# Layer norms written as (x - mean) * rsqrt everywhere, with a new stored order

## The chip, the cores and the metric

The kernel runs on one core of one Trainium2 chip. Its time is device microseconds per execution, and lower is better. A core has five engines that run side by side: TensorE (PE, matmuls, with its weight loads shown as PEld), VectorE (DVE), ScalarE (ACT), GpSimd (POOL) and SyncE (SP, which here issues nearly all the DMAs). They wait for one another through semaphores alone. TensorE writes into eight PSUM banks, and all other tiles lie in SBUF, 128 partitions wide.

## The reference

A transformer block whose two norms are modulated by a condition vector `c`. With S = 2048 tokens and D = 448, it computes

```
sa, ca, ga, sb, cb, gb = split(silu(c) @ w_mod, 6)
h = layernorm(x) * (1 + ca) + sa
x = x + ga * attention(h)            # 16 heads of 28, causal, window of 256 keys
h = layernorm(x) * (1 + cb) + sb
z = gelu(h @ w_in)                   # 448 -> 1792
z1, z2 = z[:, :896], layernorm(z[:, 896:])
x = x + gb * ((z1 * (w_sp @ z2 + b_sp)) @ w_out)      # w_sp is 2048 x 2048
```

where `layernorm(v) = (v - mean) / sqrt(var + 1e-5)` along the last axis, with no gain or offset of its own. Inputs and output are bf16.

## The kernel before

The 2048 tokens are 16 tiles of 128 rows (`NT`). All stages run interleaved on all engines.

- First norm (`ln1`). The tiles are grouped in blocks of 1, 1, 2, 4, 4 and 4 (`BLOCKS`). For each tile VectorE computes statistics (`bn_stats`, named `l1_<t>st0`) and aggregates them to mean and variance (`l1_<t>ag`, into `mv_all`). For each block one operation adds epsilon (`l1_<t0>ve`, into `ve_all`, VectorE) and one raises to the power -0.5 (`l1_<t0>rs`, into `rs_all`, GpSimd). From the second block on a further operation makes -mean * rsqrt (`l1_<t0>nm`, into `nm_all`, VectorE). The norm of a tile (`xn<t>`, into `xn`) then runs on one of the engines that its list of options has: on VectorE as subtract and multiply, on GpSimd as multiply and add of `nm_all`, on ScalarE as an Identity activation with scale and bias.
- Transposing the normed tiles to hT: for the first three blocks by matmuls against an identity (`tr<b>_...`), evicted with the modulation (`hT<b>_<u>`); for the three blocks of four tiles by DMA transposes on SP's queue (`hx<t>`, line 717), followed by the modulation in place (`hm<b>_<c>`, line 707), four of them to a block, each on an engine of choice.
- Projections (`qk<b>_<g>`, `v<t>`), evicted by ScalarE or VectorE (`qke<b>_<g>`, `ve<t>`); scores (`S...`), exponentials on ScalarE (`E...`, line 887), masks on GpSimd (`M...`, line 890), the product with V (`PV...`), and per tile on VectorE or GpSimd a transpose, a reciprocal and a scaling (`oq<j>`, `rec<j>`, `nrm<j>`, `oT<j>`); then the output projection (`wo<j>`) and its addition to x (`x1_<j>`).
- Second norm (groups of 4, 4, 4, 2 and 2 tiles): the same statistics and the same helper `ln_rs`, with `l2_<j0>nm` always; the norm itself (`x2_<j>`) in the multiply-and-add form on all three engines; DMA transposes (`h2T<j>`), modulation (`h2q...`, `h2m...`).
- The gated MLP: `z2m`, `z1m` (matmuls), `z2g`, `z1g` (gelu on ScalarE), the third norm per tile (`l3_<t>...`, `z2n<t>`, already in the subtract-and-multiply form), then `G<tb>_<ft>_<qd>` (the product with w_sp, whose transposed blocks are loaded by `wsp<tb>_<p>`), and `out`, `fin`, `st`. Matmuls on 64 of 128 rows (names that end in `_r`) can run two at a time when the two use opposite halves and stand next to each other.

What sets the order. Every operation is declared with its dependencies and its options (engine, cost). Nothing is planned when the kernel is built: `ORDER` is a text that lists all operations by number in their order of issue, with the option taken after a dot (none is the first) and the buffers or banks taken after a slash. `Planner.schedule` reads it; each engine then runs its own operations in that order, each waiting for what it depends on. So an operation that waits holds back everything behind it on its engine, SP's DMAs too. TensorE's operations are of several shapes of its array (whole, 32 columns wide, 28 or 64 rows high), and neighbours in the order share a shape where they can.

Of the kernel before, what the change touches and what calls it, by code (L numbers as in the profile page):

```python
# [179 lines left out]
1 34 32 31 0 2 3 4 8 11 23 27 22 33 24 25 28 21 29 1693/0 1694 1695 1696 1697 1698 36 35 37/0 1699 1700 1701 15 67 38 1702 39 40/6 41 42 43 26 68 69  # L180
70 71/2 44 45 46 47 48 49 50 51 52 53 54 55 72/0 76/7 56 73 77.1 78/2 79.1 1703 74/4 1704 57.1 75 6 65.1 60.1 7 61.1 5 64.1 1705 1706 1707 1708 1709
12 18 10 9 62.2 125 126 127 63.2 58.2 180 182 128 129 181 95/7 96 85/0 90/1 91 80/2 105/3 81 86 115/6 106 97 98 82 87 88 92 93 99 83 89 94 116 107 117
118 119 108 109 130/2 133/4 134 131/7 183 66 184 1710 84.1 496/0,0 498/1 1711 1712 132.1 150/1 135/0 165/2 140/3 141 136 151 152 59.2 137 153 154 166
138 167 142 168 139 143 144 251 169 110/2 111 100/3 112 113 114 101 102 103 104 145/1 146 147 148 149 155/3 156 157 158 160/0 161 159 162 163 164
497/1,1 501/9 170/2 171 172 173 185 186 188.1/0 187.1/3 189/1 190 192/3 193 194 30.1 247 245 249 246 248 252 250 253 254 120/6 121 122 123 174.1
513/0,1 514/4 517/6 175/2 176 177 13 19 14 494/3 178 179 191.1 255 256/0 124.1 332 225/1 215/0 227 226 218 228 229 520/1,0 523/5 521/7 217 16 17 495
20 260 195/2 198 197 196 199.1 205/1 206 216 219.1 207 208 209.1 330 333 328 334 331 329 335 336 200/3 202 203 201 204 220/2 221 223 222 224 230/0 231
# [12 lines left out]
668 666 664 375.1 401/1 665 675/0 676 404 403 694/3 696/2,1 697 402 405.1 677/1 626/0 627 628 629 630 946 953.1/1 699 698 700 454/1 701/0,2 705/0 455  # L200
456 457 458.1 674/0 669 671 673 672 670 684/0 706/1 702/2 703/4 708/1,2 709/1 678/1 391/1 394 392 393 395.1 685 686/0 449/0 451 450 710/0 704 707
711/1,0 714 715 712 713 679/1 687/2 680 681 682 683 961 464/3 466 444/2 465 467.1 468.1 452.1 453 447.1 746/0,1 748/4 917 918 911 1428 1425 954 916
446 445 448.1 727/0 434/1 726 722 725 723 724 747/2 749/1,2 752 949/0 947/1 737/0 951/2 962 738 436 435 437 438.1 739.1/1 750 751 753 688/0 689 690
691 692 740/2 959 963 964 965 960 754/0,2 755/3 459/1 719/0 462.1 718 721 460 720 756/0 758/1 759/2 757 760 761/1,0 762/0 763/5 966 461 463.1 479/2
481 469/3 472 470 716 717 728/0 729 967 482 480 483 764/1,0 765 471 473.1 484/0 486 485 439/1 487 488.1 441 767 799/2,1 800/3 730.1/0 731/0 921 1426
919 920 910 950 952 948 1432 1431 909 1429 440 442 443.1 766 768 801/1 956.1 769/0 773 770 772 771 774 781/0 968 958 955 957 802/0,2 805 806 741/1 742
782 732/0 733 734 735 736 969 783/0 976.1/0 977 803 804 807/2,1 743 744 778/0 780 775 745 784/0 811/4 812/1 808/2 809/0 813 814/1,0 816/4 776 777 779
790/0 791 785/1 786 787 788 789 792/1 815/0 817/0,2 818 1433 1436 810 820 474/0 475 477 476 478.1 931/1 852/0,1 854/5 853/2 825/0 823 822 826 1035/2
1036 1037 793/1 935 794/3 795 934 819 824 821 827 834/0 796 797 798 835 932 933 1038 1043.1 970/0 971 974/2 972/1 973 855/0,1 858 856 1052/0 1053 1054
1069/3 1071 1039/2 1070 1040 1041 1072 1077.1 1042 1044 982 984 986 988 1055 1060.1 857 836.1/0 859 837/2 860/0,1 1090/3 1056/1 1091 1092 830/0 833  # L210
489/2 490 491 1057 1058 831 864/3 865/4 861/2 866 862/1 863 1093 1095.1 492.1 493.1 1059 1061.1 867/0,1 868/1 975 978.1 828 829 832 843/0 838/3 839
840 841 1086/1 1087 1088 842 987 985 989 983 990 991 869/3 1073/0 1074 1089 1076 1094.1 870/2,0 873 1430 1434 1438 871 1096/0 844 980 845/0 979 1075
846/2 1078 981.1 992 995/2 996 999.1/1 993.1/0 1000 994 1295/6 1305/7 1296 1307 1306 1300/3 1297 1301 1154/0 1150 1302 1330/1 1332 1333 1298 1303 1304
1153 1308 1309 1157 847/2 848 1005 1156 849 1155 850 851 1006 1007 1331 1151 1152 1103/1 1104 1158/2 872 874 879/0 1107/2 1340/7 876 880 875 878 877
1109 1097 1008 1009 887/0 1160 1335/4 1337 1110 1338 1343 1106 1334 1299 1079/1 997/2 888 1010 1011 1098 1080 1081 1159 998 1014/1 889.1/0 1015 1315/1
885/0 1105 1108 1112.1 1111.1 1336 1339 882 883 1317 1320/6 1012.2/0 1013 881 1316 1321 884 1310/0 1312 886 1453 1451 1441 1440 1445 1442 890/2 896/0
897 1082 1161 1162 898/0 1083 1120/0 1342 1124 1322 1325/3 1127 1318 1319 1313 1123 1323 1328 891/0 892 1341 893 894 895 1125 1290/1 1126 1326 1344
1324 1121 1122 1291 1311 1128/3 1002.2 1314 1004.1 1084 1163 1099 899/0 900/0 901 902 1292 1020 1001 903 904 1164 1085 1370/7 1180/0 1181 1327 1375/6
1371 1182 1003.2 1045/1 1329 1365/0 1376 1366 1184 1186 1185 1293 1294 1368 1373 1378 1187 1183 1188/2 1372 1367 1380/3 1350/1 1381 1369 1377 1374
1379 1382 1355/2 1199/0 1357 1195 1197 1285/0 1286 1356 1200 1165/1 1169 1172 1198 1383 1288 1353 1358 1202 1168 1170 1196 1201 1171 1021 1016 1022  # L220
1017.2 1100 1130 1023 1024 1129 1101 1025 1131 1026 1029.2/0 1384 1027.1/2 1102 1132 1133 1046 1047 1048 1049 1028 1134 1190 1189 1191 1359 1203/0
1167 1352 1287 1166 1345/3 1360/2 1214/0 1215 1210 1216 1212 1351 1173/3 1289 1354 1211 1361 1225/1 1229 1019.1 1050 1018.1 1348 1217 1363 1228 1051
1192 1205 1030 1455 1034.2 1213 1232 1218/1 1227 1362 1226 1032.1 1031.1 1385/0 1230 1347 1364 1033.1 1259/0 1193 1175 1204 1174 1219 1194 1176 1177
1220 1178 1179 1206 1221 1222 1207 1208 1223 1255 1346 1349 1231 1257 1260 1233/2 1386 1387 1395/2 1397 1390/3 1391 1135/1 1139 1062/3 1064 1235 1224
1209 1063 1065 1066 1388 1389 1142 1393 1138 1258 1262 1392 1394 1261 1256 1137 1405/1 1141 1410/0 1140 1136 1143/1 1412 1400/3 1401 1407 1396 1411
# [72 lines left out]
def bass_adaLN_cond__sliding_block__mixer_gmlp__prompt_kernel(  # L298
# [14 lines left out]
    FH = 896  # L313
# [300 lines left out]
    def ln_rs(name, prio, slot, t0, n, deps, nm):  # L614
# [4 lines left out]
        if not nm:  # L619
            return r  # L620
# [19 lines left out]
    def ln1(b, pr):  # L640
# [8 lines left out]
        for t in range(t0, t0 + n):  # L649
# [12 lines left out]
            if b:  # L662
                opts += [("pool", pool2_ns(512), f_p)] + ([("act", act_ns(512), f_a)])
# [640 lines left out]
```

## Time and profile before

| | us |
|---|---|
| median of three runs | 265.88 (265.82 to 266.1) |
| the profiled execution | 265.4 |
| its span, from the first instruction to the last | 263.7 |
| TensorE busy in it | 257.2 |
| VectorE busy | 164.3 |
| ScalarE busy | 128.8 |
| GpSimd busy | 95.2 |

The profile is one execution. A line of a group reads: source line, engine, operation, out<-in, shapes, count, then busy time and mean duration in ns, then idle time of the engine just before and what ended it. A line of a timeline reads: start, length (both us), engine, line, operation, count, and in brackets the idle time before it with the engine that ended it. Names are the program's tiles, so operations of different names can share a line (707 is a modulation, 630 a norm in the multiply-and-add form, 631 one in the subtract-and-multiply form, 616 the epsilon addition, 617 the power, 621 and 647 the l_nm operations). SPq is SP's queue of DMA issues.

### The profile page before, as it was taken

The numbers are of one execution on the slowest core, as the hardware profiler recorded it, in microseconds if no ns is written. First come the engines' busy times: TensorE is split into PE (matmuls) and PEld (weight loads), VectorE is DVE, ScalarE is ACT, GpSimd is POOL, SyncE is SP. The second block draws the span as 40 slices with busy tenths as digits, with TensorE's granted clock in tenths as the row PEclk, the third lists the DMA queues.
The fourth block names the chain that finished last, engine by engine and source line by source line (L and its number), as shares of the span: only waits on it lengthen the run. The fifth ranks groups of instructions, "written<-read, shape, count | busy, mean of one in ns | idle before, by whom it ended". The sixth has DMA issues, their size and how long they took to land.

```text
span 263.7 us, 7760 instructions
## 1 busy us (share of the span) xinstructions
PE 257.2 (98%) x3395; PEld 128.7 (49%) x3395; DVE 164.3 (62%) x387; ACT 128.8 (49%) x183; POOL 95.2 (36%) x148
## 2 busy tenths in 40 slices
PE   6999999999999999999999999999999999999996
PEld 2675455655455554543434444444444444444453
DVE  4798988788989997979587702352514213344453
ACT  4899999999999999778888000000000000000000
POOL 3594968878878776515331300000000000000000
DMA  6975560256994764768899400000000000000043
GB/s 225 357 193 120 145 163 5 62 125 145 227 114 118 118 87 101 85 130 154 144 199 222 92 2 0 0 0 2 0 0 0 2 0 0 0 2 17 0 142 119
DMA packets 61022, 23.86 MB, mean 91 GB/s; under 512 B 49854, under 2 KB 60861, under 8 KB 60989
## 3 DMA queue, kind: packets, MB, share of 16 engines
q1 hardware_dynamic: 60715, 22.92, 40.0%
q8 instruction: 26, 0.43, 0.6%
q10 hardware_dynamic: 274, 0.46, 0.5%
q14 instruction: 7, 0.06, 0.1%
HBM read 9.47 MB, written 1.84 MB: 43 GB/s over the span
## 4 chain that ended last, share of the span: by engine, by line
PE 91%; DVE 3%; POOL 2%; ACT 1%; DMA 1%; issue 1%; SPq 0%; DVEq 0%; POOLq 0%
PE ps L467 80%; PE ps L464 11%; DVE hT L707 1%; DMA hT<-xn 1%; ACT arena L887 1%; POOL xn L630 1%; POOL arena L890 0%; ACT WQK L734 0%; DVE x_sb L1077 0%; SPq L717 0%; DVE QKT L820 0%; ACT hT L693 0%; PE ps L779 0%; DVE xn L630 0%; DVE o_sb L1063 0%
## 5 line engine op out<-in xcount | busy, mean ns | idle before, releaser
L887 ACT ACTIVATE arena<-ps 128x1024 bf16<-128x1024 f32 x76 | 72.4, 1028 | 2.0 <-PE ps L467 1.4
L1212 DVE TENSOR_TENSOR tmpg<-ps,bsp_bc 128x512 bf16<-128x512 f32 x28 | 19.2, 689 | 60.2 <-PE ps L467 59.9
L467 PE MATMUL ps<-QKT,z 128*128 128x512 bf16 x224 | 52.1, 379 | 0.0
L890 POOL TENSOR_SCALAR_AFFINE_SELECT arena<-arena 128x512 f32<-128x512 f32 x60 | 39.1, 669 | 12.2 <-ACT arena L887 9.5
L467 PEld LDWEIGHTS ps<-QKT,z 128*128 128x128 bf16 x224 | 21.9, 98 | 26.4
L617 POOL TENSOR_TENSOR rs_all<-ve_all,neghalf 128x1 f32<-128x1 f32 (+2 forms) x27 | 18.9, 703 | 33.1 <-DVE ve_all L616 32.9
L467 PE MATMUL ps<-w_spD,z 128*128 128x512 bf16 x112 | 27.9, 379 | 0.0
L467 PE MATMUL ps<-w_spC,z 128*128 128x512 bf16 x112 | 27.8, 379 | 0.0
L467 PE MATMUL ps<-hT,w_in_sb 128*128 128x512 bf16 (+1 forms) x97 | 25.3, 380 | 0.0
L467 PE MATMUL ps<-w_in_sb,hT 128*128 128x448 bf16 (+1 forms) x102 | 24.6, 353 | 0.0
L467 PE MATMUL ps<-w_out_sb,z1T 128*128 128x448 bf16 (+2 forms) x119 | 22.0, 341 | 0.0
L609 DVE BATCH_NORM_STATS2 st_all<-z2raw 128x6 f32<-128x448 bf16 x32 | 18.7, 616 | 4.9 <-ACT z2raw L1135 3.9
L467 PE MATMUL ps<-hT,WQK 128*128 128x128 bf16 (+4 forms) x124 | 19.9, 291 | 0.1
L609 DVE BATCH_NORM_STATS2 st_all<-x_sb 128x6 f32<-128x448 bf16 x32 | 18.6, 608 | 0.0
L467 PE MATMUL ps<-QKT 28*64 28x64 bf16 (+3 forms) x944 | 17.7, 210 | 0.6 <-ACT arena L887 0.3
L1154 ACT ACTIVATE z1T<-ps 128x512 bf16<-128x512 f32 x28 | 15.9, 597 | 4.3 <-PE ps L467 4.2
L467 PE MATMUL ps<-arena,Vaug 128*32 128x128 bf16 x720 | 17.7, 221 | 0.0
L467 PEld LDWEIGHTS ps<-w_spC,z 128*128 128x128 bf16 x112 | 11.0, 98 | 13.2
L467 PEld LDWEIGHTS ps<-w_spD,z 128*128 128x128 bf16 x112 | 11.0, 98 | 13.0
L467 PEld LDWEIGHTS ps<-QKT 28*128 28x128 bf16 (+1 forms) x944 | 11.3, 97 | 11.7 <-ACT arena L887 5.9
L630 POOL TENSOR_SCALAR xn<-x_sb,rs_all,nm_all 128x512 bf16<-128x512 bf16 x20 | 15.4, 781 | 4.0 <-DVE nm_all L647 1.7
L467 PEld LDWEIGHTS ps<-w_out_sb,z1T 128*128 128x128 bf16 x119 | 11.6, 98 | 10.1
(93 smaller groups left out, 331.7 us busy)
## 6 DMA issues: line engine op xcount, KB each, us to landing
wmod_sb<-in_w_mod_dram SPq DMA_DIRECT2D x8, 224.0 KB, 3.8
w_in_sb<-in_B_w_in_dram SPq DMA_DIRECT2D x8, 224.0 KB, 4.0
out_dram<-fin SPq DMA_DIRECT2D x16, 112.0 KB, 1.7
x_sb<-in_A_x_dram SPq DMA_DIRECT2D x3, 448.0 KB, 8.1
bsp_bc<-in_B_b_sp_dram SPq DMA_DIRECT2D x1, 512.0 KB, 4.0
wqk_raw<-in_A_wqkv_dram SPq DMA_DIRECT2D x1, 452.0 KB, 5.7
wmod_sb<-in_w_mod_dram SPq DMA_DIRECT2D x1, 448.0 KB, 4.9
wmod_sb<-in_w_mod_dram ACTq DMA_DIRECT2D x1, 448.0 KB, 5.0
```

What stands on the lines that cost most here:

```text
L464: last = e.matmul(out_[32 * j:32 * j + 32], lhsT=lhsT[:, 32 * j:32 * j + 32], rhs=rhs, start=st, stop=sp, tile_position=(0, 32 * j), **kw)
L467: return e.matmul(out_, lhsT=lhsT, rhs=rhs, start=st, stop=sp, **kw)
L609: st = [dve("%sst%d" % (name, i), prio, dve_ns(D), lambda e, i=i, s_=s_: e.bn_stats(st_all[:, slot, t, i, :], s_()), deps, tens) for i, s_ ...
L617: r = pool(name + "rs", prio, 420 + 148 * n, lambda e: e.tensor_tensor(rs_all[:, slot, t0:t1], ve_all[:, slot, t0:t1], neghalf[:, t0:t1], ...
L630: return e.tensor_scalar(dst, src, rs_all[:, slot, t:t + 1], nm_all[:, slot, t:t + 1], ALU.mult, ALU.add)
L707: return e.tensor_scalar(hT[:, c_, cols], hT[:, c_, cols], modT[:, base_col + 4 + c_:base_col + 5 + c_], modT[:, base_col + c_:base_col + ...
L887: return P.op(name, pr, [("act", 925, lambda e: e.activation(e_out(), e_in(), ACT.Exp, scale=SCALE))], [s_op, t_exp0], tens + [pt], table= ...
L890: return pool(name, pr, pool_ns(n), lambda e: e.affine_select(out=pt32(slot_out.slot, off, dims), in_=pt32(slot_in.slot, off, dims), patte ...
L1154: g = P.op("z1g%d_%d" % (tb, ft), pr - 19, [("act", act_ns(512), lambda e: e.activation(z1T[:, ft, tb * 512:(tb + 1) * 512], ps[:, ten.slo ...
L1212: a = dve("ga%d_%d" % (tb, ft), pr, dve_ns(512), lambda e, tb=tb, ten=ten, tg=tg: e.tensor_tensor(tmpg[:, tg.slot, :], ps[:, ten.slot, :], ...
```

## The change

The norm is written as subtract and multiply on every engine. With that, the operations `l..nm` and the tile `nm_all` are dropped (five `l1_..nm` and five `l2_..nm`; 1713 operations become 1703), and ScalarE is no longer an option for `xn` and `x2`, since it would need `nm_all` as its bias. The epsilon addition `..ve` gets GpSimd as a second option.

```diff
-    def ln_rs(name, prio, slot, t0, n, deps, nm):
+    def ln_rs(name, prio, slot, t0, n, deps):
         t1 = t0 + n
-        v = dve(name + "ve", prio, 75, lambda e: e.tensor_scalar(ve_all[:, slot, t0:t1], mv_all[:, slot, t0:t1, 1], EPS, None, ALU.add), deps)
-        r = pool(name + "rs", prio, 420 + 148 * n, lambda e: e.tensor_tensor(
+        def ve_fn(e):
+            return e.tensor_scalar(ve_all[:, slot, t0:t1], mv_all[:, slot, t0:t1, 1], EPS, None, ALU.add)
+        v = P.op(name + "ve", prio, [("dve", 75, ve_fn), ("pool", 110, ve_fn)], deps)
+        return pool(name + "rs", prio, 420 + 148 * n, lambda e: e.tensor_tensor(
             rs_all[:, slot, t0:t1], ve_all[:, slot, t0:t1], neghalf[:, t0:t1], ALU.pow), [v, t_nh])
-        if not nm:
-            return r
-        return dve(name + "nm", prio, 75, lambda e: e.scalar_tensor_tensor(
-            nm_all[:, slot, t0:t1], mv_all[:, slot, t0:t1, 0], -1.0, rs_all[:, slot, t0:t1], ALU.mult, ALU.mult), [r])
...
-    def norm(e, slot, t, dst, src, nm):
-        if nm:
-            return e.tensor_scalar(dst, src, rs_all[:, slot, t:t + 1], nm_all[:, slot, t:t + 1], ALU.mult, ALU.add)
+    def norm(e, slot, t, dst, src):
         return e.tensor_scalar(dst, src, mv_all[:, slot, t, 0:1], rs_all[:, slot, t:t + 1], ALU.subtract, ALU.mult)
...
-            opts = [("dve", dve4_ns(512), f_d)]
-            if b:
-                opts += [("pool", pool2_ns(512), f_p)] + ([("act", act_ns(512), f_a)])
+            def f_n(e, t=t, ten=ten):
+                return norm(e, 0, t, xnv(xn, ten.slot), spread(x_sb[:, t, :]))
+            opts = [("dve", dve4_ns(512), f_n)] + ([("pool", pool2_ns(512), f_n)] if b else [])
...
-                                        ("act", act_ns(512), lambda e, j=j, x2t=x2t: e.activation(
-                                            xnv(xn2, x2t.slot), spread(x_sb[:, j, :]), ACT.Identity, bias=nm_all[:, 1, j:j + 1], scale=rs_all[:, 1, j:j + 1]))],
-                      [rs], [x2t], port=True)
+            x2 = P.op("x2_%d" % j, pr, [("pool", pool2_ns(512), f_n), ("dve", dve4_ns(512), f_n)], [rs], [x2t], port=True)
```

`ORDER` is replaced as a whole. Its first tokens (the numbers are those of the operations, in their new count on the + line):

```diff
-1 34 32 31 0 2 3 4 8 11 23 27 22 33 24 25 28 21 29 1693/0 1694 1695 1696 1697 1698 36 35 37/0 1699 1700 1701 15 67 38 1702 39 40/6 41 42 43 26 68 69
+0 27 1 21 22 25 24 23 28 32 2 3 4 8 6 7 11 1683/0 1684 1685 1686 1687 1688 35 34 36 15 67 68 69.1 37/3 1689 1690 1691 1692 33 38 40/4 41 42 39 43 44
...
```

Read by name, the two texts give each engine the following. TensorE has the same 892 operations, in an order that differs in places while the scores, exponentials and PV products follow in nearly the same sequence. VectorE goes from 385 operations to 362, GpSimd from 144 to 161, ScalarE from 180 to 176. Of the 27 epsilon additions 22 are on GpSimd (five of the first norm, four of the second, 13 of the third). These operations change engine beside them: `xn1` and `xn4` go from VectorE to GpSimd; `xn6` to `xn9` from GpSimd, and `xn10` from ScalarE, to VectorE; `xn15` and `x2_12` from ScalarE to GpSimd, `x2_15` from ScalarE to VectorE, `x2_3` and `x2_14` from VectorE to GpSimd; the modulations `hm4_2`, `hm4_3`, `hm5_2`, `hm5_3` from GpSimd to VectorE; `hT0_3` from VectorE to ScalarE; some weight copies, evictions (`qke`, `ve`) and products (`nrm`) between VectorE, ScalarE and GpSimd, in both directions.

In the start VectorE's new order is `modAe`, `l1_1st0`, `l1_1ag`, `hT0_2`, three weight copies, `l1_2st0`, `l1_3st0`, `l1_2ag`, `hT1_0`, `qke0_7`, `l1_3ag`, the statistics of tiles 4 to 7, `zv` (a memset), `qke1_7`, `hT2_0`, `xn6`, `xn7`. GpSimd's is `l1_1ve`, `l1_1rs`, `xn1`, three weight copies, `l1_2ve`, `l1_2rs`, `xn3`, `xn2`, `l1_4ve`, `l1_4rs`, `xn5`, a mask, `xn4`. SP's first transposes come as `hx6`, `hx5`, `hx7`, `hx4` instead of `hx4`, `hx5`, `hx7`, `hx6`, and the next four follow directly, ahead of the loads `wmod3` and `wmod4` which stood between. `wqkR0` and `wqkR1` are issued before `x1` (tiles 2 and 3), `x4` (tiles 12 to 15) before `x3` (tiles 8 to 11), `wsp0_3` at the end of the attention instead of in its middle.

More of the change, by code (lines that the diff above doesn't have):

```diff
@@ L184 @@
[L184 to L187, printed above, removed]
@@ L236 @@
[L236 to L238 removed]
+0 27 1 21 22 25 24 23 28 32 2 3 4 8 6 7 11 1683/0 1684 1685 1686 1687 1688 35 34 36 15 67 68 69.1 37/3 1689 1690 1691 1692 33 38 40/4 41 42 39 43 44
+45 46 47 48 49 50 51 52 53 54 55 70 71/4 31 26 74/0 78/7 72/2 56 73 79 1693 1694 1695 1696 1697 76/6 1698 75 1699 1700 90/3 80/2 91 1701 62.2 63.1
@@ L239 @@
+1682
 """
@@ L356, in bass_adaLN_cond__sliding_block__mixer_gmlp__prompt_kernel @@
     rs_all, _, _ = alloc("rs_all", [128, 3, NT], F32)
-    nm_all, _, _ = alloc("nm_all", [128, 3, NT], F32)
     rec_all, _, _ = alloc("rec_all", [128, NT, H], F32)
@@ L643, in ln1 @@
         if b == 0:
-            r = [ln_rs("l1_%d" % (t0 + i), pr, 0, t0 + i, 1, [ags[i]], False) for i in range(n)]
+            rs = [ln_rs("l1_%d" % (t0 + i), pr, 0, t0 + i, 1, [ags[i]]) for i in range(n)]
         else:
-            r = [ln_rs("l1_%d" % t0, pr, 0, t0, n, ags, False)]
-        rs = r if b == 0 else [dve("l1_%dnm" % t0, pr, 75, lambda e: e.scalar_tensor_tensor(
-            nm_all[:, 0, t0:t0 + n], mv_all[:, 0, t0:t0 + n, 0], -1.0, rs_all[:, 0, t0:t0 + n], ALU.mult, ALU.mult), r)] * n
+            rs = [ln_rs("l1_%d" % t0, pr, 0, t0, n, ags)] * n
         for t in range(t0, t0 + n):
@@ L651, in ln1 @@
             xn_ten[t] = ten
-            def f_d(e, t=t, ten=ten):
-                return norm(e, 0, t, xnv(xn, ten.slot), spread(x_sb[:, t, :]), False)
-            def f_p(e, t=t, ten=ten):
-                return norm(e, 0, t, xnv(xn, ten.slot), spread(x_sb[:, t, :]), True)
-            def f_a(e, t=t, ten=ten):
-                return e.activation(xnv(xn, ten.slot), spread(x_sb[:, t, :]), ACT.Identity, bias=nm_all[:, 0, t:t + 1], scale=rs_all[:, 0, t:t + 1])
-            opts = [("dve", dve4_ns(512), f_d)]
-            if b:
-                opts += [("pool", pool2_ns(512), f_p)] + ([("act", act_ns(512), f_a)])
+            def f_n(e, t=t, ten=ten):
+                return norm(e, 0, t, xnv(xn, ten.slot), spread(x_sb[:, t, :]))
+            opts = [("dve", dve4_ns(512), f_n)] + ([("pool", pool2_ns(512), f_n)] if b else [])
             xn_op[t] = P.op("xn%d" % t, pr + 0.1, opts, [rs[t - t0]], [ten], port=True)
@@ L1089, in bass_adaLN_cond__sliding_block__mixer_gmlp__prompt_kernel, with f_n @@
         ags = [ln_stats("l2_%d" % j, pr, 1, j, [lambda j=j: x_sb[:, j, :]], [x1_op[j]]) for j in js]
-        rs = ln_rs("l2_%d" % j0, pr, 1, j0, n, ags, True)
+        rs = ln_rs("l2_%d" % j0, pr, 1, j0, n, ags)
         for j in js:
             x2t = Ten(rot("x2", NX2))
-            x2 = P.op("x2_%d" % j, pr, [("pool", pool2_ns(512), lambda e, j=j, x2t=x2t: norm(e, 1, j, xnv(xn2, x2t.slot), spread(x_sb[:, j, :]), True)),
-                                        ("dve", dve4_ns(512), lambda e, j=j, x2t=x2t: norm(e, 1, j, xnv(xn2, x2t.slot), spread(x_sb[:, j, :]), True)),
-                                        ("act", act_ns(512), lambda e, j=j, x2t=x2t: e.activation(
-                                            xnv(xn2, x2t.slot), spread(x_sb[:, j, :]), ACT.Identity, bias=nm_all[:, 1, j:j + 1], scale=rs_all[:, 1, j:j + 1]))],
-                      [rs], [x2t], port=True)
+            def f_n(e, j=j, x2t=x2t):
+                return norm(e, 1, j, xnv(xn2, x2t.slot), spread(x_sb[:, j, :]))
+            x2 = P.op("x2_%d" % j, pr, [("pool", pool2_ns(512), f_n), ("dve", dve4_ns(512), f_n)], [rs], [x2t], port=True)
             h2_raw[j] = P.op("h2T%d" % j, pr, [("sp", 1250, lambda e, j=j, x2t=x2t: e.dma_start_transpose(
```

114 lines of the change are left out of this document (58 added, 56 removed).

## The prediction

> **What bounds the kernel now.** I read the page first, then busy time in stretches that I cut at the visible pauses of TensorE, then the chain that ended last, and last the timelines of single engines where the chain leaves TensorE. The page has one engine full:
>
> ```profile
> PE 257.2 (98%) x3395; PEld 128.7 (49%) x3395; DVE 164.3 (62%) x387; ACT 128.8 (49%) x183; POOL 95.2 (36%) x148
> ```
>
> The stretches say where TensorE pauses at all (the first column of numbers is the stretch's length, then each engine's busy time and its instructions in brackets: PE, PEld, DVE, ACT, POOL):
>
> ```profile
> 7.50:12.80 5.30, 4.74 (x105) 2.81 (x102) 4.87 (x18) 4.83 (x15) 3.54 (x6) 1.00 1.11 354
> 12.80:27.00 14.20, 13.70 (x212) 8.87 (x216) 12.80 (x36) 13.90 (x27) 9.41 (x13) 1.00 0.65 167
> 27.00:73.00 46.00, 46.00 (x1303) 25.43 (x1304) 39.59 (x85) 43.97 (x51) 38.14 (x53) 1.00 0.53 125
> 73.00:86.00 13.00, 12.37 (x408) 7.07 (x405) 11.66 (x28) 12.55 (x15) 10.51 (x15) 1.00 0.72 108
> 86.00:261.10 175.10, 175.07 (x1355) 82.25 (x1347) 92.16 (x213) 50.41 (x73) 31.17 (x48) 1.00 0.31 60
> ```
>
> TensorE pauses 0.56 us (5.30 - 4.74) in the start, 0.50 up to 27 us, 0.63 between 73 and 86, and 0.03 in the 175 us after that. The granted clock, third number from the right, is 1.00 throughout. A matmul's record runs on past its turn (further down, one of 0.36 at 23.79 against 0.92 for four of the same width at 15.80), so a pause shows 0.1 to 0.2 us too short; all together the pauses are some 2 to 4 us. That is all that a better order can win besides a shorter TensorE program, and all norms together sit in it or nowhere. Who ends the pauses, the chain tells:
>
> ```profile
> 10.93 0.41 DVE xn L631
> ...
> 21.38 0.94 SPq L717
> ...
> 22.36 2.60 DMA hT<-xn
> ...
> 25.16 1.74 DVE hT L707 x4
> ...
> 112.42 148.67 PE ps L467 x729
> ```
>
> So the norms matter twice: the second tile's norm (10.93), and the norms of tiles 4 to 7, behind which four transposes stand on SP's queue. The last 148.67 us are TensorE alone; there the 13 epsilon additions of the last norm that change engine cost nothing, since TensorE waits for nobody, up to some 0.03 us of pause.
>
> **The change, start.** Ten l_nm operations go (five of the first norm, five of the second; the change's title counts eleven). VectorE's and GpSimd's timelines of the start:
>
> ```profile
> 7.66 0.17 DVE L594 TENSOR_TENSOR modT<-ps,zero_one 128x8 f32<-128x8 f32 x1 [2.23 <-PE ps L467]
> 7.94 0.73 DVE L698 TENSOR_SCALAR hT<-ps,modT 128x128 bf16<-128x128 f32 x2
> 8.59 0.62 DVE L609 BATCH_NORM_STATS2 st_all<-x_sb 128x6 f32<-128x448 bf16 x1
> 9.24 0.18 DVE L612 BATCH_NORM_AGGREGATE mv_all<-st_all 128x2 f32<-128x6 f32 x1
> ...
> 12.00 0.72 DVE L698 TENSOR_SCALAR hT<-ps,modT 128x128 bf16<-128x128 f32 x2
> ...
> 13.23 1.67 DVE L609 BATCH_NORM_STATS2 st_all<-x_sb 128x6 f32<-128x448 bf16 x3
> 14.82 0.36 DVE L612 BATCH_NORM_AGGREGATE mv_all<-st_all 128x2 f32<-128x6 f32 x4
> 15.22 0.17 DVE L616 TENSOR_SCALAR ve_all<-mv_all 128x4 f32<-128x4 f32 x1
> ...
> 15.78 1.00 DVE L698 TENSOR_SCALAR hT<-ps,modT 128x256 bf16<-128x256 f32 x2
> 16.69 0.41 DVE L647 SCALAR_TENSOR_TENSOR nm_all<-mv_all,rs_all 128x4 f32<-128x4 f32 x1
> 17.20 0.41 DVE L631 TENSOR_SCALAR xn<-x_sb,mv_all,rs_all 128x512 bf16<-128x512 bf16 x1
> ```
> ```profile
> 9.70 0.55 POOL L617 TENSOR_TENSOR rs_all<-ve_all,neghalf 128x1 f32<-128x1 f32 x1 [0.47 <-DVE ve_all L616]
> 15.47 1.01 POOL L617 TENSOR_TENSOR rs_all<-ve_all,neghalf 128x4 f32<-128x4 f32 x1
> ```
> ```profile
> 17.65 5.98 SPq L717 DMA_TRANSPOSE hT<-xn  x4
> ```
> ```profile
> 12.78 2.18 PE L467 MATMUL ps<-hT,WQK 128*128 128x128 bf16 x36
> 15.80 0.92 PE L467 MATMUL ps<-wv_sb,hT 128*128 128x448 bf16 x4
> 25.62 0.40 PE L464 MATMUL ps<-hT,WQK 128*32 128x512 bf16 x4 [0.37 <-DVE hT L707]
> ```
>
> Second tile. Its statistics stand behind two hT evictions now (8.59); the new order puts them right behind the modT row, which ends at 7.83. The 8.59 row has no wait in front of it, so nothing shows that its load landed later than VectorE came; if it did land only then, 0.76 of what follows is lost. New: statistics 7.83 to 8.45, aggregate to 8.65, then epsilon, rs and now xn1 too on GpSimd. The epsilon addition there has no row; it lies between the memset of four columns and the 256-wide scalar operation. The norm has one (the three numbers of L630 are shortest, median and longest, in ns):
>
> ```profile
> L539 POOL MEMSET zero_one<- 128x4 f32 x2 | 0.2, 102 | 0.3 <-POOLq L1289 0.3
> L707 POOL TENSOR_SCALAR hT<-hT,modT 128x256 bf16<-128x256 bf16 x5 | 2.7, 554 | 1.6 <-DMA hT<-xn 1.6
> L630 POOL TENSOR_SCALAR xn<-x_sb,rs_all,nm_all x20: 764/768/908, 13.4 to 108.9; 128x512 bf16<-128x512 bf16 x20
> L630 DVE TENSOR_SCALAR xn<-x_sb,rs_all,nm_all x5: 412/737/791, 63.3 to 121.1; 128x512 bf16<-128x512 bf16 x5
> ```
>
> I take 0.2, nearer to the small one (on VectorE the four-wide one above is 0.17). [...] Then xn1 ends at 8.65 + 0.1 + 0.2 + 0.55 + 0.77, about 10.3, where it ends at 11.34 now. VectorE next does one hT eviction (half of the 0.73), three small weight copies (priced like the aggregates, 0.2 each), two statistics (a third of 1.67 each), an aggregate, and the hT pair that sits at 12.00: 8.65 + 0.4 + 0.6 + 1.1 + 0.2 = 10.95, plus 0.72 = 11.7. TensorE's row 12.78 starts about 1 us sooner; ScalarE's evictions, as dense as now, will let some 0.7 of it through.
>
> Tiles 4 to 7. Four statistics of 0.56 and aggregates of 0.36 follow a small eviction and an aggregate (0.5, an estimate from the small rows above): 11.7 + 0.5 + 2.2 + 0.4 = 14.8 (now 15.18). Epsilon and rs on GpSimd: 14.8 + 0.1 + 0.2 + 1.0 = 16.1 (now 16.48). Now the l_nm row waits behind the hT pair and takes 0.41, and the norm starts at 17.20. In the new order VectorE has a memset and a small eviction (0.6 together, estimated likewise) and the hT pair (1.0) from 14.8 to 16.4, then goes straight into two norms of 0.41: the first transposes at 16.85, not at 17.65, so 0.8 sooner. The other two norms come from GpSimd at about 17 and 18.3, long before SP has issued two transposes (5.98 for four). Behind it the chain is serial (SP 5.98, landing 2.60, hT 0.41), so row 25.62 moves by the same 0.8. Low end: 0.3, when the load or ScalarE holds the start; high end: 1.05.
>
> **TensorE's program.** Read from the two stored orders, the same 892 operations remain. Half-height matmuls that stand beside their opposite half run at the same time:
>
> ```profile
> 23.79 0.36 PE L467 MATMUL ps<-wv_sb,hT 64*128 64x448 bf16 x1
> 23.79 0.39 PE L467 MATMUL ps<-hT,WQK 64*128 64x256 bf16 x2
> ```
>
> There are 35 such pairs now and 37 in the new order; a 448-wide pass takes 0.23 (0.92 / 4 at 15.80), so 0.4 to 0.5 less. One change of array shape more (118 for 117) takes part of it back: -0.3.
>
> **The middle, 27 to 86 us.** ScalarE loses four norms of 0.8 and gets some hT work back; VectorE and GpSimd:
>
> ```profile
> L660 ACT ACTIVATE xn<-x_sb,nm_all,rs_all 128x512 bf16<-128x512 bf16 x2 | 1.6, 822 | 0.0
> L1095 ACT ACTIVATE xn<-x_sb,nm_all,rs_all 128x512 bf16<-128x512 bf16 x2 | 1.7, 831 | 0.0
> ```
> ```profile
> 59.72 0.69 DVE L820 CAST QKT<-ps 128x512 bf16<-128x512 f32 x1 [0.38 <-PE ps L464]
> 70.96 0.72 DVE L1058 STREAM_TRANSPOSE oq<-ps 128x512 f32<-128x512 f32 x1 [0.23 <-PE ps L467]
> 77.10 0.72 DVE L1058 STREAM_TRANSPOSE oq<-ps 128x512 f32<-128x512 f32 x1 [0.77 <-PE ps L467]
> 84.51 0.40 PE L467 MATMUL ps<-QKT 28*128 28x192 bf16 x16 [0.31 <-ACT arena L887]
> ```
>
> Two of the four ScalarE norms, 1.6 us, lie ahead of the exponentials of this stage, so waits such as the 0.31 at 84.51 should go: -0.3. VectorE is given xn8 to xn10 and four hT modulations here (seven of about 0.41) and three evictions and one o_sb product (0.7 each, by 59.72), and is rid of three evictions, two products, one norm, three epsilon additions and four l_nm: close to even in sum, but the seven come bunched, and between 59.72 and 77.10 it has hardly a pause. I allow +0.4 there (none to 2.5). The norm in the new form, subtract then multiply, is on VectorE already (17.20, 0.41) and costs the same; on GpSimd I take the 0.77 of the old form, with two scalars read in either.
>
> SP: in the start two small pieces of wqk go ahead of the load of tiles 2 and 3, and tiles 12 to 15 ahead of 8 to 11; the statistics that read them lie behind other VectorE work in the new order as well, so I give this nothing (if that work does not cover it, tiles 2 and 3 hold back the 11.7 above by what they land late). Later the loads for the second modulation move behind the second four transposes, and one pair of w_sp blocks is loaded much later; where they are used TensorE's pause is 0.03, so nothing again, at the price of one landing (2.6) if that cover is gone. The end, from 261.1 to the span's 263.7, is the same.
>
> **Sum.** -0.8 - 0.3 - 0.3 + 0.4 = -1.0. The profiled execution took 265.4 with a span of 263.7, so 264.4 in its terms; the median of the three runs is 265.88, and I forecast 264.9 against that.
>
> **Rivals.** (1) VectorE becomes the bound between 60 and 86 us, and the kernel is slower. The mechanism is in the L630 rows: the same norm takes VectorE 0.41 at best and 0.74 in the median, which I read as meeting GpSimd's work. [...] Seven moved operations times 0.33 are 2.3 us, with 0.2 of sum 2.5. VectorE's pauses up to 73 us (46.00 - 39.59 = 6.4) absorb what falls early; it decides from the point where the load meets the stretch without pauses at 59.72. If four fifths of it arrive there, TensorE waits 2.0 us and the gains of 1.1 are used up (the ScalarE wait, overtaken, counts no more): +0.9, 266.8. For it: the 0.23 and 0.77 are the only waits of note there. Against it: GpSimd has less to do in the new order, so fewer meetings.
>
> (2) The start gives nothing, and the change does less than it says: the norm's subtraction was on VectorE already for three tiles, and SP's transposes turn out to be held by the loads still in flight (the DMA share, last but one in the stretches, is 1.11 up to 12.80 and 0.65 after). Then -0.3 - 0.3 + 0.4 = -0.2, 265.7.
>
> **Numbers.** About 0.5 us (0.2%) is what a measurement tells from no change. Forecast 50%, its own range 264.0 to 265.3; rival 2 20%; rival 1 30%. The range for all is 264.0 to 267.0: the high start with the ScalarE wait gone and VectorE even at the low end, rival 1 at the high end. Faster 0.50, same 0.20, slower 0.30.
>
> **What would show it.** Right: SP's first transposes at about 16.9, row 25.62 at about 24.8, no ScalarE wait near 84 us, and 86 to 261 us still without pauses. Wrong: the first transposes at 17.6 or later (rival 2), or pauses of TensorE ended by VectorE between 60 and 86 us with L630 or L707 on VectorE at 0.7 (rival 1).

## The result: 277.75 us, slower by 4.4%

The changed kernel takes 277.75 us in the median of four runs (276.72 to 278.72) against 265.88 before: a ratio of 1.0444 (95% interval 1.0406 to 1.0483). The forecast was 264.9 with a range to 267.0, so the sign and the size were both wrong, and the time lies far outside the range. The profiled execution took 278.72 with a span of 276.9.

The page after, busy time and the granted clock by slices:

```profile
PE 259.3 (94%) x3372; PEld 129.0 (47%) x3392; DVE 162.3 (59%) x364; ACT 127.0 (46%) x179; POOL 127.2 (46%) x165
...
PEclk9986999999999999999999999999999999999999
```

TensorE's work is about what it was (257.2), so most of the 13 us of span are pauses. VectorE and ScalarE have less to do, GpSimd has 32 us more (95.2 before). The view of the norm's line says why (shortest, median and longest in ns, then the first and the last start):

```profile
L626 POOL TENSOR_SCALAR xn<-x_sb,mv_all,rs_all x22: 2067/2077/2597, 10.0 to 133.9; 128x512 bf16<-128x512 bf16 x22
...
L626 DVE TENSOR_SCALAR xn<-x_sb,mv_all,rs_all x10: 397/544/864, 5.1 to 134.8; 128x512 bf16<-128x512 bf16 x10
```

The same instruction that takes VectorE 0.54 us in the median (0.40 at least) takes GpSimd 2.08; in the multiply-add form of before it took GpSimd 0.77. The other operation that moved there, the epsilon addition, costs about the 0.2 that was forecast, a little more than on VectorE before (median 0.15):

```profile
L616 POOL TENSOR_SCALAR ve_all<-mv_all x22: 208/224/383, 4.2 to 163.1; 128x1 f32<-128x1 f32 x15, 128x4 f32<-128x4 f32 x5, 128x2 f32<-128x2 f32 x2
```

The chain that ended last now goes through GpSimd's norms, up to three in a row (its other pieces are left out):

```profile
10.01 2.10 POOL xn L626
...
14.90 4.15 POOL xn L626 x2
...
53.37 6.18 POOL xn L626 x3
...
60.44 2.08 POOL xn L626
...
69.89 1.82 POOL xn L626
...
77.88 4.56 POOL xn L626 x3
...
100.40 6.18 POOL xn L626 x3
```

And the stretches (length, then PE, PEld, DVE, ACT, POOL, then granted clock, DMA share, GB/s) show what that does to TensorE:

```profile
7.50:12.80 5.30, 3.40 (x91) 2.08 (x88) 3.13 (x10) 3.35 (x12) 4.21 (x6) 1.00 1.12 336
12.80:27.00 14.20, 11.27 (x119) 6.75 (x116) 8.37 (x21) 8.88 (x20) 13.82 (x14) 0.76 0.64 126
27.00:73.00 46.00, 44.26 (x1224) 24.61 (x1226) 39.66 (x90) 41.19 (x51) 39.05 (x45) 1.00 0.43 107
73.00:86.00 13.00, 12.00 (x312) 6.18 (x313) 8.51 (x20) 12.21 (x15) 12.93 (x14) 1.00 0.65 121
86.00:112.00 26.00, 21.78 (x604) 11.56 (x604) 21.03 (x44) 21.91 (x26) 23.62 (x29) 1.00 0.33 62
```

GpSimd is busy 13.82 of 14.20 us in the start and 12.93 of 13.00 us from 73 to 86: in these places it is the bound. TensorE pauses 1.9, 2.9, 1.7, 1.0 and 4.2 us in the five stretches (0.6, 0.5, 0.0, 0.6 and 0.0 before). In the start something else is added: the granted clock falls to 0.76. TensorE's timeline shows its three waits for GpSimd's norms and what a row costs after them:

```profile
12.17 0.40 PE L466 MATMUL ps<-ident,xn 128*128 128x128 bf16 x4 [1.37 <-POOL xn L626]
...
17.13 0.38 PE L466 MATMUL ps<-ident,xn 128*128 128x128 bf16 x4 [0.91 <-POOL xn L626]
...
19.10 0.61 PE L466 MATMUL ps<-ident,xn 128*128 128x128 bf16 x4 [1.59 <-POOL xn L626]
19.50 1.70 PE L466 MATMUL ps<-wv_sb,hT 128*128 128x448 bf16 x4
```

Four 448-wide matmuls take 1.70 us at 19.50, where before took 0.92 for the same four: in this trace the granted clock is 0.50 from 18.5 to 25.3 us. It falls some 1.0 us into the longest of these waits (17.51 to 19.10); in the 5.7 us ahead of that, from 12.8, TensorE was busy for 3.36, and the wait of 1.37 us had ended at 12.17. How much idle time it takes no run here shows.

What the low clock costs can be read against a run further down, which has the same dear start and the low clock earlier: 0.95 from 7.50 to 12.80, and its 36 matmuls at 13.06 take 3.42 us, where here 36 take 2.39 at 13.28, while the four take 0.92 at 19.12. It comes out of the wait of 1.59 us 0.2 us sooner than the changed kernel (18.89 against 19.10), and reaches the last half-height matmuls of these projections 3.1 us sooner (26.84 against 29.97). So in this trace the price of waiting is not only the wait, but also the slow matmuls after it. How much of that reaches the end is not shown: the four executions of the changed kernel had a mean granted clock of 0.988, 0.988, 0.994 and 0.981, and the one with the lowest was the fastest (276.72).

### The profile page after: what moved, and what is told of

The parts are those of the page before. It is cut to its first block, busy times and chain, and to the rows that moved or that the text cites. A ratio compares the mean times of both kernels' runs of the same rounds, so it can differ in the third digit from the quotient of the medians.

```text
span 276.9 us, 7721 instructions
## 1 busy us (share of the span) xinstructions
PE 259.3 (94%) x3372; PEld 129.0 (47%) x3392; DVE 162.3 (59%) x364; ACT 127.0 (46%) x179; POOL 127.2 (46%) x165
## 4 chain that ended last, share of the span: by engine, by line
PE 69%; POOL 18%; ACT 4%; DMA 3%; issue 2%; DVE 2%; SPq 0%; POOLq 0%
PE ps L466 64%; POOL xn L626 10%; PE ps L463 6%; POOL arena L875 5%; ACT arena L872 4%; DMA x_sb<-in_A_x_dram 2%; DMA hT<-xn 1%; POOL o_sb L1048 1%; POOL rs_all L618 1%; DVE st_all L608 1%; POOL WQK L720 1%; ACT z2raw L1118 0%; DVE oT L1052 0%; POOL hT L692 0%; POOL ve_all L616 0%
## 5 line engine op out<-in xcount | busy, mean ns | idle before, releaser
L466 PE MATMUL ps<-QKT,z 128*128 128x512 bf16 x219 | 50.7, 379 | 0.3
L626 POOL TENSOR_SCALAR xn<-x_sb,mv_all,rs_all 128x512 bf16<-128x512 bf16 x22 | 46.9, 2138 | 0.6
L466 PE MATMUL ps<-w_spD,z 128*128 128x512 bf16 x110 | 26.4, 379 | 0.2
L466 PE MATMUL ps<-w_spC,z 128*128 128x512 bf16 x110 | 26.2, 379 | 0.1
L466 PE MATMUL ps<-w_in_sb,hT 128*128 128x448 bf16 (+1 forms) x104 | 25.5, 353 | 0.4 <-issue 0.2
L466 PE MATMUL ps<-hT,w_in_sb 128*128 128x512 bf16 (+1 forms) x90 | 24.0, 380 | 0.6 <-DVE x_sb L1062 0.3
L466 PE MATMUL ps<-arena,Vaug 128*32 128x128 bf16 x720 | 18.4, 221 | 3.0 <-POOL arena L875 1.6
L466 PE MATMUL ps<-hT,WQK 128*128 128x128 bf16 (+4 forms) x116 | 18.5, 288 | 0.8 <-DVE hT L683 0.4
L466 PEld LDWEIGHTS ps<-arena,Vaug 128*32 128x32 bf16 x720 | 13.5, 95 | 10.6 <-POOL arena L875 2.3
L466 PEld LDWEIGHTS ps<-QKT 28*128 28x128 bf16 (+1 forms) x944 | 11.4, 98 | 12.1 <-ACT arena L872 7.2
```

The costliest lines, as they stand in the source:

```text
L466: return e.matmul(out_, lhsT=lhsT, rhs=rhs, start=st, stop=sp, **kw)
L626: return e.tensor_scalar(dst, src, mv_all[:, slot, t, 0:1], rs_all[:, slot, t:t + 1], ALU.subtract, ALU.mult)
```

## Experiments

Theory 1: the pair of operations, subtract then multiply, is dear on GpSimd, and that alone makes the 12 us. Theory 2: the new stored order, or the epsilon additions in it, crowd GpSimd, and the long norms come of that. Theory 3: the scalar `mv_all` (every second element of a tile) is dear, not the pair.

**The old order with the dear pair.** Two lines of `norm` go (shortened here):

```
-        if nm:
-            return e.tensor_scalar(dst, src, rs_all[...], nm_all[...], ALU.mult, ALU.add)
         return e.tensor_scalar(dst, src, mv_all[...], rs_all[...], ALU.subtract, ALU.mult)
```

> The kernel before, its stored order and all its l_nm operations kept, only GpSimd's and VectorE's norms all computed as (x - mean) * rsqrt. Theory 1 (the operation pair is dear on GpSimd): each of the 20 GpSimd norms takes 2.1 instead of 0.77, 27 us more work on an engine that is busy 48.7 of the 59 us from 27 to 86 us (38.14 + 10.51), so TensorE waits for it there: 8 to 14 us slower, 274 to 280. Theory 2 (the new order, or the epsilon additions in it, make GpSimd late, and the 2.1 comes of contention in that order): the norms stay at 0.8 and the time within 1 us of before.

Measured: 285.77 us, a ratio of 1.0747 (1.0703 to 1.0790) to before. The group of GpSimd's norms (busy, mean ns):

```profile
L629 POOL TENSOR_SCALAR xn<-x_sb,mv_all,rs_all 128x512 bf16<-128x512 bf16 x20 | 41.5, 2082 | 5.8 <-DVE nm_all L645 2.8 <-DMA hT<-xn 2.6 <-DVE nm_all L621 0.3
```

With no new order and no epsilon on GpSimd the norm takes the same 2.08, so theory 2 falls. The time missed theory 1's 274 to 280 on the high side: 26 us more work in GpSimd's norms cost 20 us here. The new order bears the dear pair better than the old one, by 8 us (277.75 against 285.77).

**The new order with the cheap pair.** For GpSimd alone, whose options set `fast` (shortened here); the form adds the mean in place of its true shift, so it serves to measure time only:

```
+        if fast:
+            return e.tensor_scalar(dst, src, rs_all[...], mv_all[...], ALU.mult, ALU.add)
```

> The changed kernel with its order and its epsilon additions, but GpSimd's norms as x * rsqrt + mean (multiply, then add, with the same two scalars rs_all and mv_all), which leaves out the true shift of the norm. Theory 1: the norms fall to 0.77, and the time to what the prediction's other steps give, 264 to 266. Theory 2 (order): norms and time stay as after, 276 to 279. Theory 3 (the strided scalar mv_all is what is dear, not the pair): the norms stay at 2.1 and the time at 276 to 279.

Measured: 265.65 us (264.26 to 267.9, 12 runs), ratio 0.9995 (0.9971 to 1.0020). The norm's line in its trace:

```profile
L627 POOL TENSOR_SCALAR xn<-x_sb,rs_all,mv_all x22: 761/767/925, 10.9 to 122.2; 128x512 bf16<-128x512 bf16 x22
```

The same two scalars, `mv_all` among them, and 0.767: theory 3 falls with theory 2. All 12 us are the price of the pair: GpSimd's busy time falls from 127.2 to 98.4, so 28.8 us of work on it cost 12.1 us of time.

**Which pairs are dear.** 

> The kernel before with 18 forms of a GpSimd scalar operation, four of each in a chain, behind all its own GpSimd work, on tiles that are no longer used; the first twelve 128x512 bf16. Theory 1: subtract-then-multiply takes 2.1 with either scalar as the mean (mv_all or nm_all) and multiply-then-add 0.77; what the other pairs and the single operations take is not forecast by it, and tells whether subtraction, the order of the two, or any pair but multiply-add is dear. Theory 3: 2.1 only where mv_all is read, 0.77 with nm_all. A small multiplication of four columns should take about 0.2, as the epsilon addition does.

The groups of this run behind GpSimd's own work, in order of cost (busy, mean ns); 1257 and 1258 are subtract-multiply by `mv_all` and by `nm_all`, 1262 add-add, 1260 multiply-subtract, 1264, 1263 and 1265 a lone addition, subtraction and multiplication, 1261 multiply-multiply, 1256 multiply-add, 1259 add-multiply:

```profile
L1262 POOL TENSOR_SCALAR xn<-xn,nm_all 128x512 bf16<-128x512 bf16 x4 | 8.8, 2212 | 0.4
L1260 POOL TENSOR_SCALAR xn<-xn,rs_all,nm_all 128x512 bf16<-128x512 bf16 x4 | 8.6, 2152 | 0.4
L1258 POOL TENSOR_SCALAR xn<-xn,nm_all,rs_all 128x512 bf16<-128x512 bf16 x4 | 8.6, 2139 | 0.4
L1257 POOL TENSOR_SCALAR xn<-xn,mv_all,rs_all 128x512 bf16<-128x512 bf16 x4 | 8.3, 2083 | 0.4
...
L1264 POOL TENSOR_SCALAR xn<-xn,nm_all 128x512 bf16<-128x512 bf16 x4 | 6.8, 1700 | 0.4
L1263 POOL TENSOR_SCALAR xn<-xn,nm_all 128x512 bf16<-128x512 bf16 x4 | 6.4, 1598 | 0.4
L1265 POOL TENSOR_SCALAR xn<-xn,rs_all 128x512 bf16<-128x512 bf16 x4 | 6.3, 1566 | 0.4
L1261 POOL TENSOR_SCALAR xn<-xn,rs_all 128x512 bf16<-128x512 bf16 x4 | 3.6, 903 | 0.4
...
L1256 POOL TENSOR_SCALAR xn<-xn,rs_all,nm_all 128x512 bf16<-128x512 bf16 x4 | 3.3, 836 | 0.3
L1259 POOL TENSOR_SCALAR xn<-xn,nm_all,rs_all 128x512 bf16<-128x512 bf16 x4 | 3.1, 772 | 0.4
```

Whose scalar it is doesn't matter, and it isn't subtraction as such: add-add is as dear, and a lone operation takes twice what a quick pair takes. Nor does VectorE's work beside it make the gap: in the middle of the changed kernel (27 to 73 us) VectorE is busy for 39.66 of 46 us, from 150 to 266 us in the kernel before, where these groups stand, for 40.16 of 116, and the 2.08 is the same. Constants in place of the scalars from memory leave the gap as well: subtract-multiply 1.93, multiply-add 0.62. Add-multiply is quick, so `(x + (-mean)) * rs` is a cheap form of the very same norm. A multiplication of four columns took 0.25, near the epsilon addition's 0.22.

**More pairs and widths.** The same with 20 other forms.

> The kernel before with 20 more forms on GpSimd behind its own work, four of each. Theory (three pairs of add and multiply have a quick form and everything else, lone operations too, a slow one): subtract with add, add with subtract and subtract with subtract take 2.1 to 2.2 at 512 columns, pairs with a maximum 2.1, and a multiplication with a second one by 1.0, or with an addition of 0.0, takes 0.8 to 0.9, less than the 1.57 of the multiplication alone. By width subtract-then-multiply rises by 3.3 ns a column, (2139 - 863) / 384, to about 1.3 at 256 and 0.65 at 64; add-then-multiply by 0.5, to about 0.65 and 0.55. Rival (only a subtraction, or an addition in the second place, is slow): pairs with a maximum at 0.8.

Subtraction with addition (either way round) or with a second subtraction took 2.07 to 2.14, and the pairs with a maximum 2.07 to 2.21, as expected; the rival falls. A product with a second factor of 1.0 took 0.70, less than the 0.8 to 0.9 that was expected. Subtract-multiply (1271, 1268, 1265) and add-multiply (1272, 1269, 1266) at 512, 256 and 64 columns:

```profile
L1271 POOL TENSOR_SCALAR xn<-xn,nm_all,rs_all 128x512 bf16<-128x512 bf16 x4 | 8.3, 2072 | 0.4
...
L1268 POOL TENSOR_SCALAR xn<-xn,nm_all,rs_all 128x256 bf16<-128x256 bf16 x4 | 5.2, 1311 | 0.4
...
L1272 POOL TENSOR_SCALAR xn<-xn,nm_all,rs_all 128x512 bf16<-128x512 bf16 x4 | 3.1, 780 | 0.4
...
L1265 POOL TENSOR_SCALAR xn<-xn,nm_all,rs_all 128x64 bf16<-128x64 bf16 x4 | 2.3, 581 | 0.4
L1269 POOL TENSOR_SCALAR xn<-xn,nm_all,rs_all 128x256 bf16<-128x256 bf16 x4 | 2.2, 554 | 0.4
...
L1266 POOL TENSOR_SCALAR xn<-xn,nm_all,rs_all 128x64 bf16<-128x64 bf16 x4 | 1.8, 461 | 0.4
```

From 64 to 512 columns the slow form rises by (2072 - 581) / 448 = 3.3 ns a column, as expected, the quick one by (780 - 461) / 448 = 0.7 (0.5 was expected). Nearly all of the difference is work per column; at the one to four columns of the epsilon addition, by these slopes, a slow form costs hardly more.

**Epsilon on VectorE, with the dear pair.** `("pool", 110, ve_fn)` becomes `("dve", 75, ve_fn)`.

> The changed kernel with all 27 epsilon additions on VectorE and nothing else changed. Theory 1: the additions are not the cause, GpSimd's norms still take 2.1, the time stays within 2 us of after (275 to 279). Rival (the epsilon additions queue behind long GpSimd work and hold the norms back): most of the 12 us goes, 266 to 270.

Measured: 275.96 us (ratio 1.0387, 1.0362 to 1.0413), GpSimd's norms at 2.08 still. As theory 1 has it, the additions are only some 1.8 of the 12 us (275.96 against 277.75; the two intervals just overlap).

**Where the 12 us fall.** The dear pair in the first tiles alone (`fast and t >= 8` in the first norm), and everywhere else alone (`fast and t < 8`, and not in the second norm):

> The changed kernel with subtract-then-multiply kept for GpSimd's norms of tiles 1, 2, 3, 4 and 5 (five norms) and x * rsqrt + mean (the true shift left out) for its 17 others. Shares the 12 us between the start and the rest. Theory 1a (the start matters most: its norms stand in one chain, TensorE idles and comes back at a lower granted clock): 4 to 7 us of the 12, 270 to 273, with the granted clock under 0.9 between 14 and 27 us. Theory 1b (GpSimd full between 27 and 112 us is the cause): 1 to 3 us here, 266.5 to 269, and the most of it in the sister run.

> The complement: x * rsqrt + mean for tiles 1 to 5, subtract-then-multiply for the 17 other GpSimd norms. Theory 1a: 271 to 274 (5 to 8 us). Theory 1b: 274 to 277 (9 to 11 us). In both, the granted clock stays at 1.0 in the start, and what this run and its sister cost adds up to about 12 us; if it comes to clearly more or less, the two stages hide each other.

Measured: 269.04 us (ratio 1.0115, 1.0085 to 1.0146) and 272.35 (1.0239, 1.0213 to 1.0266), two runs each. The first lies between the ranges of 1b and 1a, a hair above 1b's, and the second in 1a's. Against 265.65 the five norms of the start cost 3.4 us and the 17 others 6.7; together 10.1 of the 12.1, so some 2 us (by the intervals, anything from 0.5 to 4) come only when both are dear. Neither form of theory 1 is right alone: a dear norm costs 0.7 us in the start and 0.4 elsewhere. The stretches, first of the one with the dear start, then of the one with the dear rest:

```profile
12.80:27.00 14.20, 12.35 (x153) 8.95 (x154) 11.17 (x28) 11.64 (x25) 13.74 (x14) 0.90 0.59 132
```
```profile
12.80:27.00 14.20, 14.06 (x216) 8.65 (x213) 13.53 (x35) 14.01 (x28) 9.97 (x14) 1.00 0.60 137
27.00:73.00 46.00, 43.38 (x1229) 23.72 (x1227) 37.11 (x79) 39.82 (x47) 42.54 (x51) 1.00 0.53 118
73.00:86.00 13.00, 10.69 (x316) 5.36 (x304) 8.88 (x22) 10.87 (x12) 12.93 (x16) 1.00 0.56 107
```

The clock stays at 1.00 where the start is cheap, and GpSimd is full (12.93 of 13.00) where the rest is dear.

**The full norm with a quick pair.** Ten operations of VectorE write -mean, each placed in the order behind the epsilon addition of a group that has norms on GpSimd (shortened here):

```
+        e.tensor_scalar(nm_all[...], mv_all[..., 0], -1.0, None, ALU.mult)
+            return e.tensor_scalar(dst, src, nm_all[...], rs_all[...], ALU.add, ALU.mult)
```

> A full form of the changed kernel with a cheap pair: ten small operations of VectorE, each right behind a group's epsilon addition, write -mean, and GpSimd's norms are (x + (-mean)) * rsqrt, add then multiply, 0.77 in the pair measurement; nothing is left out. Theory 1: the time of the run with x * rsqrt + mean, 265.65, plus at most 10 times 0.15 of VectorE where it matters: 265 to 267, against 266.0 for before. Rival: the small operations delay VectorE in the start, where each holds hT's evictions: 267 to 269.

Measured: 265.80 us, ratio 1.0001 (0.9986 to 1.0016). It gives back what the dear pair took, and is no faster than before. Its start, VectorE, then GpSimd, then SP, then TensorE, is the prediction's chain with a norm of 0.77 in it:

```profile
8.12 0.63 DVE L608 BATCH_NORM_STATS2 st_all<-x_sb 128x6 f32<-128x448 bf16 x1 [0.99 <-DMA x_sb<-in_A_x_dram]
```
```profile
10.04 0.77 POOL L627 TENSOR_SCALAR xn<-x_sb,nm_all,rs_all 128x512 bf16<-128x512 bf16 x1
```
```profile
16.97 11.68 SPq L704 DMA_TRANSPOSE hT<-xn  x5
```
```profile
25.23 0.40 PE L463 MATMUL ps<-hT,WQK 128*32 128x512 bf16 x4 [0.31 <-DVE hT L694]
```

**The load of tile 1 first.** The last form with one load ahead of another in the stored order (`... 2 3 8 4 6 7` for `... 2 3 4 8 6 7`).

> The same with one more edit: the load of tile 1 is issued ahead of the 452 KB of wqk instead of behind it. In the profile of the run with x * rsqrt + mean, tile 1 landed at 8.97 us and VectorE waited 0.72 for it, so the load and not VectorE's queue held the second tile. Theory (the load is the bound of the start): it lands by 8.0, the second norm ends 0.6 to 0.9 sooner, and the time is 0.4 to 0.9 below the sister run. Rival (wqk is the next bound: its copies wait for the load too and it lands some 0.4 later): no gain or up to 0.5 slower.

Measured: 265.88 us, ratio 1.0007 (0.9986 to 1.0029): no gain, as the rival had it. VectorE's timeline has the statistics a whole us sooner and without a wait, and the gain is lost at the hT eviction, which waits for TensorE (11.82, in the sister run 11.23):

```profile
7.12 0.62 DVE L608 BATCH_NORM_STATS2 st_all<-x_sb 128x6 f32<-128x448 bf16 x1
...
11.82 0.73 DVE L685 TENSOR_SCALAR hT<-ps,modT 128x128 bf16<-128x128 f32 x2 [1.07 <-PE ps L466]
```

Whether the late wqk is the reason, as the rival says, this trace leaves open: wqk lands 5.9 us after its issue (5.8 in the sister run), and TensorE is busy for 4.93 of the 5.30 us from 7.50 to 12.80 (4.25 in the sister run).

**Epsilon on VectorE, with the quick pair.** The two edits above together.

> The full form with -mean written by VectorE and the norms as add, then multiply, but with all 27 epsilon additions on VectorE too. With the dear pair the epsilon's place was worth 1.8 us (275.96 against 277.75), which I put down to GpSimd being full. Theory: with the cheap pair GpSimd is not full, so the place is worth nothing: within 0.5 us of the form with the epsilon on GpSimd, 265.3 to 266.3. Rival (each crossing between the engines costs the chain, so that the epsilon on GpSimd is right for its own sake): 0.5 to 1.5 us slower, 266.3 to 267.3.

Measured: 265.01 us (264.03 to 265.56, 10 runs), ratio 0.9972 (0.9957 to 0.9986). This is a little under both ranges that were expected, and 0.3% under the form with the additions on GpSimd (0.9972 against 1.0001; the two intervals, of separate comparisons, touch at 0.9986). It is the one form of all these whose interval lies under 1. Its early rows are hardly sooner than its sister's:

```profile
17.02 12.06 SPq L704 DMA_TRANSPOSE hT<-xn  x6
```
```profile
24.99 0.40 PE L463 MATMUL ps<-hT,WQK 128*32 128x512 bf16 x4
```

That the place of the additions makes this gain is not shown. In all 12 runs of the sister form the time is 2.1 to 2.2 us longer than the span from the first instruction to the last; here and in before it is 1.7 longer. So more than half of the 0.8 us between the two forms lies outside the span. The mean span is 263.65 in the sister form (264.09 in before beside it) and 263.24 here (263.89): 0.44 and 0.65 us shorter than before, too close to be told apart. What makes the difference outside the span no run shows; the run with x * rsqrt + mean, which also has its epsilon additions on GpSimd, stands at 1.8.

## Why the prediction was wrong

**The step that failed** is one half sentence of the middle: "on GpSimd I take the 0.77 of the old form, with two scalars read in either". The term was 22 x 0.77 us of work and is 22 x 2.08. The trace of before had no subtract-then-multiply on GpSimd; its nearest rows were the same pair on VectorE and another pair on GpSimd, and I took the second without bounds, while the much smaller epsilon addition got bounds on both sides. A lower row was at hand for the low end (VectorE's 0.41); a high end of twice 0.77 would have put 17 us more on GpSimd and a slower case of many us among the rivals. The cost was put on an engine that the prediction read as relieved ("GpSimd has less to do in the new order"); even with the quick pair GpSimd was busy for 98.4 us, against 95.2 before.

**Rival 1** had the right sign, but the wrong engine: VectorE's norms had a median of 0.54, less than the 0.74 that it reckoned with, and GpSimd became the bound. That the 0.74 comes of meeting GpSimd's work is not shown: in before the three L630 norms of VectorE at 0.74 to 0.79 (63.29, 83.87, 102.39) ran while GpSimd was busy for 80% or more of their time, but so did one of 0.415 (102.06); the other quick one, 0.412 at 121.07, ran with GpSimd idle. **Rival 2** (265.7) is close to what the new order gives with a quick pair, 265.65, but by luck: its reason, transposes held back to 17.6 by loads, did not come about (16.97).

**The start, -0.8.** With 2.08 in it, the second norm ended at 12.11 instead of 10.3. With the quick pair it ended at 10.81: the load was not there at 7.83. The prediction had named this ("if it did land only then, 0.76 of what follows is lost"), but gave it no weight in the sum; in the profiles with this order of loads the statistics that waited for it started between 7.87 and 8.99. Then the first transposes came at 16.97 (forecast 16.85) and the 25.62 row at 25.23 (forecast 24.8): the chain came to the transposes nearly when it was forecast, and half of the 0.8 arrived.

**TensorE's program, -0.3.** No trace here shows it. The last piece of the chain is the same in both orders, first before and then the full form with a quick pair:

```profile
112.42 148.67 PE ps L467 x729
```
```profile
112.37 148.69 PE ps L466 x725
```

The 0.4 us won at 25 us is 0.05 at 112 in these two traces: it was lost between.

**The middle, -0.3 and +0.4.** TensorE's waits in the form with x * rsqrt + mean, from 25.5 to 112 us (in all, times, longest):

```profile
PE ps L463 <- DVE hT L694: 0.6, 2, 0.4
PE ps L466 <- issue: 0.4, 1, 0.4
PE ps L463 <- DVE oT L1054: 0.3, 1, 0.3
PE ps L466 <- ACT arena L874: 0.2, 1, 0.2
PE ps L463 <- DVE QKT L807: 0.2, 1, 0.2
```

A ScalarE wait of 0.2 stands where 0.31 stood, so a third of that gain came; VectorE's waits (hT, oT, QKT) are 1.1 us, where before had 0.6 in this stretch (0.4 for hT, 0.2 for oT), which is close to the +0.4. Without the dear pair the whole came to -0.1 where I had -1.0, and the interval of that ratio (0.9971 to 1.0020) leaves out the forecast's 264.9 / 265.88 = 0.9963: apart from the pair, the sum was too hopeful by about 0.9 us. Where they went is not shown. The load of tile 1 came later than the sum had it, but the run with that load first gained nothing. The place of the epsilon additions was counted at nothing where they move; the last two forms differ by 0.8, but more than half of that lies outside the span. Inside it the full form with the quick pair is 0.4 us shorter than before, so some of the forecast gain of 1.0 is there.

**What would show it** looked for pauses ended by VectorE between 60 and 86 us, and for none after. Between 60 and 86 us two pauses, 1.6 us in all, were ended by masks on GpSimd, which the list did not name, and only 0.2 by VectorE. After 86, where none was forecast, there were 4.2 us of pauses, most of them ended by VectorE; in the chain its operations stand there behind GpSimd's masks, products and the three norms at 100.40.

## To carry to other kernels

A price belongs to an engine and an operation's whole form (here 0.77 us for multiply-add and 2.08 for subtract-multiply on GpSimd, where VectorE's least in before is 0.41 for either): when an edit changes the pair of arithmetic operations in an instruction, the old form's duration on that engine is no row for the new one, and wants a bound on each side like any unknown. Where a tuned kernel carries an extra small operation that seems to be waste (here -mean * rsqrt, so that the large one could multiply and add), ask what form of the large one it buys. Here the quick form can be had off the chain: -mean needs only the mean, and the norm is then (x + (-mean)) * rsqrt.

## What the runs showed of the hardware

- GpSimd's scalar operation at 128x512 bf16 with at least one scalar from memory has a quick form for multiply-add, add-multiply and multiply-multiply (0.69 to 0.90 us) and a slow one for every other pair that was measured (2.07 to 2.21); a lone addition, subtraction or multiplication takes 1.57 to 1.70, so a multiplication with a useless second factor of 1.0 (0.70) is twice as quick as without. On VectorE the least of either pair is 0.412 in the kernel before.
- Neither form's time falls in proportion to the columns: subtract-multiply took 581, 1311 and 2072 ns at 64, 256 and 512 columns, add-multiply 461, 554 and 780. With two constants multiply-add took 621 at 512. The quick forms take 1.5 to 2.2 times VectorE's 0.41, the slow ones about five times as long. Why only three pairs are quick no run here shows.
- TensorE's granted clock fell where TensorE waited in the start: from 12.8 to 27 us it was 0.76 in the changed kernel, 0.90 with the dear pair in the start alone, and 1.00 with a cheap start. Not every wait brought this: the 4.2 us of pauses between 86 and 112 us of the changed kernel left it at 1.00, and so did a wait of 2.2 us in the start of the old order with the dear pair.
